# Inputs laid out anew on the host: linear attention with gates, queries and keys turned, token weights turned, and another order

## The chip, the core and the metric

The kernel runs on one core of a Trainium2 chip. The metric is the device time of one execution in microseconds; the layout of inputs on the host is not part of it. Names of engines: PE multiplies matrices, DVE, ACT and POOL work along rows, SP issues transfers.

## The reference

Four batches, 768 positions, 8 heads of 48 make 384 columns. Three networks follow one another: gated linear attention, softmax attention of four experts with a top-2 gate, and a token mixer with complex weights.

```python
def _attn_ref(q, k, v, f_logit):
    f = 1.0 / (1.0 + np.exp(-f_logit))
    for t in range(S):
        state = f[:, :, t, :, None] * state + np.einsum('bhd,bhe->bhde', k[:, :, t], v[:, :, t])
        y[:, :, t] = np.einsum('bhd,bhde->bhe', q[:, :, t], state)

def _moe_ref(x, w_gate, wq, wk, wv, wo):            # top 2 of 4 experts per token
    for e in range(E):
        a = softmax(causal(scale * (x @ wq[e]) @ (x @ wk[e]).T))
        out += weight_of_e * (a @ (x @ wv[e]) @ wo[e])

def _moe2_ref(x, w_theta, w_tok_r, w_tok_i, w_ch):
    theta = x @ w_theta
    y = w_tok_r @ (x * np.cos(theta)) + w_tok_i @ (x * np.sin(theta))
    u = x + y
    return u + np.maximum(u @ w_ch, 0.0)
```

The weights of the third network arrive as 64-bit numbers; the rest is float32.

## The kernel before, in words

Positions are cut into six tiles of 128 rows per batch, 24 tiles in all. Most products are made of two parts, a rounded high one and the low rest (names ending in h and l), with three products for one.

**Gla**, the linear attention. `load` brings a tile of gates (`g_f`), queries, keys and values, 128 positions on partitions, each row in runs of 48 numbers. `gate` makes logarithms of the gates on ACT and splits them (L289, L291); `cum` sums them along positions by two products with a triangle (L297, L298), takes exponentials both ways on ACT and scales keys and queries on DVE (L307, L308), and sends the decay at the tile's end through a small transfer to `g_end` (L310). `dec` turns that on PE (L324). `tr` turns keys and queries, four blocks each (L335), copied by ACT. `att` multiplies them (L348), POOL masks (L355). `out` sums values by the masked products (L366) and adds the running state's part (L370); ACT copies the result to `g_x`. `state` multiplies keys and values (L389) and updates the running state with DVE (L396, L398).

**Moe**, the softmax attention. `turn_x` turns the tile's output (L497) and splits it (`m_xh`, `m_xl`); `val` makes values and gate logits (L509), `qk` queries and keys of a pair of tiles (L556). Then 96 units (batch, expert, row tile): `score` (L604 to L607), maxima on DVE (L613), exponentials on ACT (L626), `turn` of the weights (L663) with split (L668, L675), `av` (L686, L688), `sum`, and `mix` (L723), which stores the third network's input `t_dram`.

**Weights** converts the 64-bit weights in pieces of 128 x 384 (four DVE steps L107 to L112 and one on ACT) and stores them (`w_f` to `w_dram`): 24 pieces of token weights, three of `w_ch`; three of `w_theta` stay on the chip.

**Late** and **Moe2**, the third network. `turn_rows` (L242) turns the token weights, 128 x 768 at a time, on PE and splits them from PSUM. `rot` makes the rotated inputs; `tok` multiplies (L824), `ch_a` and `ch_b` (L836, L847) finish. `Late` prepares most of the weights while the last units of the second network run.

What sets the order: `plan` gives every step a time from the table `TUNE`, sorts them, and the tool chain's scheduler places the instructions of each engine; PSUM has eight banks of one pool for all steps, and tiles in SBUF have fixed numbers of buffers. Each engine then works its instructions strictly in order; all transfers are issued by SP in order.

## Time and profile before

| | us |
|---|---|
| median of three runs | 684.59 (682.04 to 685.06) |
| the profiled execution | 685.65 |
| its span, first to last instruction | 683.9 |
| mean granted clock of PE | 0.983 |

Busy shares are taken over the whole span. A chain of waits is read backwards from the last instruction: at each point it names the work that the end waited for. [...]

### The profile page before, as it was taken

The numbers are of one execution on the slowest core, as the hardware profiler recorded it, in microseconds if no ns is written. First come the engines' busy times: TensorE is split into PE (matmuls) and PEld (weight loads), VectorE is DVE, ScalarE is ACT, GpSimd is POOL, SyncE is SP. The second block draws the span as 40 slices with busy tenths as digits, with TensorE's granted clock in tenths as the row PEclk, the third lists the DMA queues.
The fourth block names the chain that finished last, engine by engine and source line by source line (L and its number), as shares of the span: only waits on it lengthen the run. The fifth ranks groups of instructions, "written<-read, shape, count | busy, mean of one in ns | idle before, by whom it ended". The sixth has DMA issues, their size and how long they took to land.

```text
span 683.9 us, 13350 instructions
## 1 busy us (share of the span) xinstructions
PE 646.6 (95%) x4804; PEld 611.1 (89%) x4804; DVE 479.8 (70%) x1276; ACT 448.8 (66%) x1160; POOL 95.6 (14%) x118
## 2 busy tenths in 40 slices
PE   6999899999999999899999999999999999999995
PEld 5979789889889889899989998888999999999995
DVE  6289999999998999887777875987676244222221
ACT  4468778888888778887788776888877074040000
POOL 1410030000001010010000000001563042040000
PEclk8699999999999999999999999999999999999998
DMA  9387465363468264236121101245724121000110
GB/s 166 77 179 172 103 155 159 72 180 100 136 136 213 59 176 115 59 72 128 35 60 36 59 25 47 94 150 195 232 71 127 48 69 58 35 13 24 36 47 28
DMA packets 129562, 67.45 MB, mean 99 GB/s; under 512 B 107984, under 2 KB 120784, under 8 KB 129488
## 3 DMA queue, kind: packets, MB, share of 16 engines
q1 hardware_dynamic: 129488, 66.51, 37.9%
q8 instruction: 40, 0.66, 0.4%
q14 instruction: 34, 0.28, 0.1%
HBM read 47.00 MB, written 19.46 MB: 97 GB/s over the span
## 4 chain that ended last, share of the span: by engine, by line
PE 69%; DVE 17%; ACT 7%; DMA 3%; issue 3%; POOL 1%; DVEq 0%; SPq 0%; ACTq 0%; POOLq 0%
PE M L824 21%; PE M L723 6%; PE M L847 6%; PE M L366 5%; PE M L556 4%; PE M L348 3%; PE M L663 3%; PE M L370 2%; PE M L509 2%; PE M L335 2%; DVE m_m L613 2%; DVE m_al L675 2%; PE M L389 2%; PE M L604 2%; PE M L686 2%
## 5 line engine op out<-in xcount | busy, mean ns | idle before, releaser
L355 POOL TENSOR_SCALAR_AFFINE_SELECT g_a<-g_a 128x512 f32<-128x512 f32 x48 | 35.7, 761 | 360.4 <-ACT g_a L352 360.4
L626 ACT ACTIVATE m_a<-M,m_m 128x384 f32<-128x384 f32 (+4 forms) x128 | 69.9, 552 | 16.1 <-DVE m_m L613 9.5
L675 DVE TENSOR_TENSOR m_al<-M,m_ah 128x384 fp32r<-128x384 f32 (+3 forms) x128 | 62.4, 501 | 7.4 <-ACT m_ah L668 6.4
L613 DVE TENSOR_REDUCE m_m<-M 128x1 f32<-128x384 f32 (+4 forms) x128 | 62.2, 501 | 7.2 <-PE M L607 3.2
L94 ACT CAST t_uh<-M 128x384 fp32r<-128x384 f32 x24 | 11.4, 476 | 82.1 <-PE M L836 82.1
L663 PE MATMUL M<-c_ident,m_a 128*128 128x128 f32 x336 | 53.2, 275 | 4.7 <-DVE m_kl L578 4.0
L668 ACT CAST m_ah<-M 128x384 fp32r<-128x384 f32 (+3 forms) x128 | 53.4, 447 | 6.2 <-PE M L663 5.4
L366 PEld LDWEIGHTS M<-g_v,g_a 128*128 128x128 f32 x384 | 48.6, 203 | 3.2 <-POOL g_a L355 1.8
L366 PE MATMUL M<-g_v,g_a 128*128 128x48 f32 x384 | 49.7, 284 | 1.6 <-POOL g_a L355 1.0
L686 PE MATMUL M<-m_ah,m_v 128*128 128x256 f32 x192 | 48.1, 283 | 0.8 <-ACT m_ah L668 0.8
L824 PE MATMUL M<-t_z1h,t_w 128*128 128x384 f32 x138 | 46.6, 337 | 0.0
L95 DVE TENSOR_TENSOR t_ul<-M,t_uh 128x384 fp32r<-128x384 f32 x24 | 13.4, 557 | 44.5 <-ACT t_uh L94 44.4
L604 PE MATMUL M<-m_ks,m_qs 128*128 128x384 f32 (+4 forms) x128 | 44.1, 346 | 0.3 <-ACT m_a L626 0.3
L663 PEld LDWEIGHTS M<-c_ident,m_a 128*128 128x128 f32 x336 | 37.9, 141 | 6.9 <-PE M L607 3.0
L688 PE MATMUL M<-m_al,m_v 128*64 128x256 f32 x192 | 41.7, 266 | 0.7 <-DVE m_al L675 0.7
L605 PE MATMUL M<-m_kl,m_qs 128*128 128x384 f32 (+4 forms) x128 | 41.3, 324 | 0.3 <-DVE m_kl L578 0.3
L850 DVE SCALAR_TENSOR_TENSOR t_o<-M,t_u 128x384 f32<-128x384 f32 x24 | 13.4, 556 | 39.8 <-PE M L847 39.8
L129 POOL TENSOR_TENSOR t_z0l<-t_ra,t_z0h 128x384 fp32r<-128x384 f32 x23 | 24.3, 1058 | 98.3 <-ACT t_z0h L128 95.8
L686 PEld LDWEIGHTS M<-m_ah,m_v 128*128 128x128 f32 x192 | 36.2, 188 | 1.3 <-ACT m_ah L668 1.0
L723 PE MATMUL M<-m_wh,m_yh 128*128 128x384 f32 x96 | 34.7, 361 | 1.6 <-ACT m_yh L711 1.5
L723 PE MATMUL M<-m_wh,m_yl 128*128 128x384 f32 x96 | 32.4, 339 | 0.0
L723 PE MATMUL M<-m_wl,m_yh 128*128 128x384 f32 x96 | 32.3, 336 | 0.0
(245 smaller groups left out, 1994.5 us busy)
## 6 DMA issues: line engine op xcount, KB each, us to landing
t_dram<-m_xt SPq DMA_DIRECT2D x24, 384.0 KB
w_dram<-w_f SPq DMA_DIRECT2D x27, 192.0 KB
g_f<-in_f_logit_dram SPq DMA_DIRECT2D x24, 192.0 KB
g_k<-in_k_dram SPq DMA_DIRECT2D x24, 192.0 KB
g_q<-in_q_dram SPq DMA_DIRECT2D x24, 192.0 KB
g_v<-in_v_dram SPq DMA_DIRECT2D x24, 192.0 KB
w_d<-in_moe_w_tok_r_dram SPq DMA_DIRECT2D x12, 384.0 KB
w_d<-in_moe_w_tok_i_dram SPq DMA_DIRECT2D x12, 384.0 KB
```

Of the source, the lines that this page charges most:

```text
L366: nc.tensor.matmul(y[:, h * D:(h + 1) * D], t.a[:, r, hp, :], t.v[:, h * D:(h + 1) * D], start=h == 0, stop=c == 0, skip_group_check=True)
L604: nc.tensor.matmul(ps, qs[:, rows], ks[:, cols], start=True, stop=False)
L605: nc.tensor.matmul(ps, qs[:, rows], kl[:, cols], start=False, stop=not last)
L613: nc.vector.tensor_reduce(m, ps, axis=AX.X, op=OP.max, negate=True)
L626: self.nc.scalar.activation(a[:, cols], ps, AF.Exp, bias=t.m, accum_out=st.den[:, c, i % 2, e % 2:e % 2 + 1])
L663: nc.tensor.transpose(ps[:, (j - j0) * P:(j - j0 + 1) * P], t.a[:, j * P:(j + 1) * P], self.k.ident)
L668: nc.scalar.copy(hi, pv)
L675: self.nc.vector.tensor_tensor(lo, pv, hi.bitcast(F32), op=OP.subtract)
L686: nc.tensor.matmul(ps[:, o:TQ], st.v[j][:, e].rearrange("p c h -> p (c h)"), t.aT[0][:, j, o:], start=j == 0, stop=True, skip_group_check= ...
L688: nc.tensor.matmul(ps[:HD, o:TQ], st.v[j][:, e, 0, :], t.aT[1][:, j, o:], start=False, stop=True, skip_group_check=True)
L723: nc.tensor.matmul(ps[:, :DM], st.y[pr, t // 2][a][:, o], self.wl[c][:, 2 * w0 + pr, :], start=n == 0, stop=n == 5)
L824: nc.tensor.matmul(ps, self.wT[c][h][g][:, s, j * P:(j + 1) * P], self.Z[b, s][c][l], start=s == 0 and n == 0, stop=s == NT - 1 and n == 5)
```

## The change

Inputs are laid out on the host so that the first network needs less turning. Gates, queries and keys of a tile come turned: head columns on partitions (two heads of 48 in two halves of 64), positions along rows, 2 KB to a partition. The running sum of the gates' logarithms is then a scan along rows on DVE (`tensor_tensor_scan`, listed in the order as SCALAR_TENSOR_TENSOR), broken at the borders of four head pairs by `g_inside`. The decay at a tile's end is a column of that (`g_dec`), so the small transfer, the search for the least value and the turning go. Only keys are turned, for the state, and not in a batch's last tile. Outputs are made turned, in halves of 64 columns, from values padded to 64; the state is kept as a block with zeros (`g_block`), copied there by ACT. `turn_x` splits the product straight from PSUM; the fourth pair's columns (`m_x3`) go to their places by six transfers per tile on SP, and the rows of the experts' weights are laid out to suit. The token weights come turned, so `turn_rows` goes and the splits read SBUF. `w_o` also comes turned. Eight of twelve token pieces are prepared by `Late`, four by `Moe2` (before: nine and three). `TUNE` has other numbers, among them fewer warming products (46, 11 and 4 for 53, 25 and 6).

```diff
-N1 = 3
+NS0 = 4
...
-        elif it[0] == "turn":
-            _, c, t = it
-            turn_rows(self.nc, self.k, self.pM, self.raw.pop(it), [w[t // G] for w in self.wT[c]], t)
-
-
-def turn_rows(nc, k, pM, r, dst, t):
-
-    o = slice((t % G) * P, (t % G + 1) * P)
-    for h in range(2):
-        ps = pM.tile([P, 512], F32, name="M")
-        for j in range(G):
-            s = h * G + j
-            nc.tensor.transpose(ps[:, j * P:(j + 1) * P], r[:, s * P:(s + 1) * P], k.ident)
-        pv = ps[:, :DM].rearrange("p (j m) -> p j m", j=G)
-        split(nc, pv, dst[0][:, h * G:(h + 1) * G, o], dst[1][:, h * G:(h + 1) * G, o])
+        elif it[0] == "tok":
+            _, c, s = it
+            split(self.nc, self.raw.pop(it), self.wT[c][0][s], self.wT[c][1][s])
...
-        self.padded = dict(q=[], k=[])
-        for nm, n in (("q", 2), ("k", 3)):
-            for j in range(n):
-                w = self.wk.tile([P, H, HD], F32, name=f"g_{nm}{j}")
-                nc.vector.memset(w, 0.0)
-                self.padded[nm].append(w)
-        self.ends = []
-        for j in range(2):
-            w = self.wk.tile([P, 2, HD], F32, name=f"g_end{j}")
-            nc.gpsimd.memset(w, 1.0)
-            self.ends.append(w)
-        self.low = self.wk.tile([NP, B * NT], F32, name="g_low")
+        self.inside = self.wk.tile([P, NP, P], F32, name="g_inside")
+        nc.gpsimd.memset(self.inside, 1.0e30)
+        nc.gpsimd.memset(self.inside[:, :, 0:1], 0.0)
+        self.dec = self.wk.tile([P, B * NT, NP], F32, name="g_dec")
+        self.block, self.inblock = [], {}
+        for j in range(3):
+            w = self.wk.tile([P, NP, 2, HD], F32, name=f"g_block{j}")
+            nc.gpsimd.memset(w, 0.0)
+            self.block.append(w)
         self.states, self.ready = {}, {}
         self.T = {}
 
     def load(self, nm, b, c):
         t = self.T.setdefault((b, c), Bag())
-        if nm in "qk":
-            ws = self.padded[nm]
-            w = ws[(b * NT + c) % len(ws)]
-            dst = w[:, :, :D]
-        else:
-            w = self.wk.tile([P, DM], F32, name=f"g_{nm}", bufs=2)
-            dst = w.rearrange("p (h d) -> p h d", h=H)
-        self.nc.sync.dma_start(dst, self.src[nm][b, :, c * P:(c + 1) * P, :].rearrange("h t d -> t h d"))
-        setattr(t, nm + "raw" if nm in "qk" else nm, w)
+        w = self.wk.tile([P, H, HD] if nm == "v" else [P, NP, P], F32, name=f"g_{nm}", bufs=2)
+        self.nc.sync.dma_start(w, self.src[nm][b, c])
+        setattr(t, nm, w)
...
     def gate(self, b, c):
         nc, t = self.nc, self.T[b, c]
-        g = self.wk.tile([P, DM], F32, name="g_g")
-        nc.scalar.activation(g, t.f, AF.Exp, scale=-1.0)
-        nc.scalar.activation(g, g, AF.Ln, bias=1.0)
-        yield
-        t.gh = self.wk.tile([P, DM], F32R, name="g_gh")
-        nc.vector.tensor_scalar(t.gh, g, GCLAMP, None, op0=OP.min)
-        t.gl = self.wk.tile([P, DM], F32R, name="g_gl")
-        nc.vector.scalar_tensor_tensor(t.gl, g, GCLAMP, t.gh.bitcast(F32), op0=OP.min, op1=OP.subtract)
+        nc.scalar.activation(t.f, t.f, AF.Exp, scale=-1.0)
+        nc.scalar.activation(t.f, t.f, AF.Ln, bias=1.0)
+        yield
+        t.cum = self.wk.tile([P, NP, P], F32, name="g_cum")
+        flat = lambda a: a.rearrange("p n t -> p (n t)")
+        nc.vector.tensor_tensor_scan(flat(t.cum), flat(self.inside), flat(t.f), initial=0.0, op0=OP.min, op1=OP.add)
 
     def cum(self, b, c):
         nc, t = self.nc, self.T[b, c]
-        i = b * NT + c
-        ps = self.pM.tile([P, 512], F32, name="M")
-        nc.tensor.matmul(ps[:, :DM], self.k.upper_r, t.gh, start=True, stop=False)
-        nc.tensor.matmul(ps[:, :DM], self.k.upper_r, t.gl, start=False, stop=True)
-        yield
-        ei = self.wk.tile([P, DM], F32, name="g_ei")
-        nc.scalar.activation(ei, ps[:, :DM], AF.Exp)
-        e = self.wk.tile([P, DM], F32, name="g_e", bufs=2)
-        nc.scalar.activation(e, ps[:, :DM], AF.Exp, scale=-1.0)
-        yield
-        heads = lambda a: a.rearrange("p (h d) -> p h d", h=H)
-        k, q = t.kraw[:, :, :D], t.qraw[:, :, :D]
-        (nc.vector if i < 2 or TUNE['e_k'] else nc.gpsimd).tensor_tensor(k, k, heads(ei), op=OP.mult)
-        (nc.vector if i < 2 or TUNE['e_q'] else nc.gpsimd).tensor_tensor(q, q, heads(e), op=OP.mult)
-        t.k, t.q, t.end = t.kraw, t.qraw, self.ends[i % 2].rearrange("n j d -> n (j d)")
-        nc.sync.dma_start(self.ends[i % 2][:NP, :, :D], e[P - 1:P, :].rearrange("p (n j d) -> p n j d", n=NP, j=2))
-
-    @staticmethod
-    def pair(a, hp):
-        return a[:, 2 * hp:2 * hp + 2, :].rearrange("p h d -> p (h d)")
-
-    def dec(self, b, c):
+        ei = self.wk.tile([P, NP, P], F32, name="g_ei")
+        nc.scalar.activation(ei, t.cum, AF.Exp)
+        e = t.f
+        nc.scalar.activation(e, t.cum, AF.Exp, scale=-1.0)
+        yield
+        nc.vector.tensor_tensor(t.k, t.k, ei, op=OP.mult)
+        nc.vector.tensor_tensor(t.q, t.q, e, op=OP.mult)
+        (nc.vector if TUNE['e_dec'] else nc.gpsimd).tensor_copy(self.dec[:, b * NT + c, :], e[:, :, P - 1])
...
-        nc.vector.tensor_copy(t.dec[:, :, 0], ps[:, :NP])
-
-    def tr(self, b, c):
-        nc, t = self.nc, self.T[b, c]
-        bank = {}
-        for nm in "kq":
-            ps = bank[nm] = self.pM.tile([P, 512], F32, name="M")
-            for hp in range(NP):
-                nc.tensor.transpose(ps[:, hp * P:(hp + 1) * P], self.pair(getattr(t, nm), hp), self.k.ident)
-        yield
-        for nm, ps in bank.items():
-            sb = self.wk.tile([P, NP, P], F32, name=f"g_{nm}T")
-            (nc.vector.tensor_copy if TUNE['e_' + nm + 'T'] else nc.scalar.copy)(sb.rearrange("p n t -> p (n t)"), ps)
-            setattr(t, nm + "T", sb)
+        for hp in range(NP):
+            nc.tensor.transpose(ps[:, hp * P:(hp + 1) * P], t.k[:, hp, :], self.k.ident)
+        yield
+        t.kn = self.wk.tile([P, H, HD], F32, name="g_kn")
+        (nc.vector.tensor_copy if TUNE['e_kn'] else nc.scalar.copy)(t.kn.rearrange("p h d -> p (h d)"), ps)
...
-                nc.tensor.matmul(ps[:, hp, :], t.kT[r, hp, :], t.qT[r, hp, :], start=True, stop=True)
+                nc.tensor.matmul(ps[:, hp, :], t.k[r, hp, :], t.q[r, hp, :], start=True, stop=True)
...
-        y = self.pM.tile([P, 512], F32, name="M")
-        for r in range(2):
+        y = self.pM.tile([P, NP, P], F32, name="M")
+        for hp in range(NP):
+            for r in range(2):
+                nc.tensor.matmul(y[64 * r:64 * r + 64, hp, :], t.v[:, 2 * hp + r, :], t.a[:, r, hp, :],
+                                 start=hp == 0, stop=c == 0, skip_group_check=True)
+        if c > 0:
+            assert self.inblock[(b * NT + c - 1) % 3] == (b, c)
+            bd = self.block[(b * NT + c - 1) % 3].rearrange("p n r d -> p n (r d)")
             for hp in range(NP):
-                h = 2 * hp + r
-                nc.tensor.matmul(y[:, h * D:(h + 1) * D], t.a[:, r, hp, :], t.v[:, h * D:(h + 1) * D],
-                                 start=h == 0, stop=c == 0, skip_group_check=True)
-        for hp in range(NP):
-            if c > 0:
-                nc.tensor.matmul(y[:, hp * 96:(hp + 1) * 96], t.qT[:, hp, :], self.states[b][:, hp, :],
-                                 start=False, stop=True, skip_group_check=True)
+                nc.tensor.matmul(y[:, hp, :], bd[:, hp, :], t.q[:, hp, :], start=False, stop=True, skip_group_check=True)
         t.used = True
-        yield
-        x = self.x[b, c] = self.wk.tile([P, DM], F32, name="g_x")
-        (nc.vector.tensor_copy if TUNE['e_x'] else nc.scalar.copy)(x, y[:, :DM])
+        self.x[b, c] = y
...
-            st = self.states[b] = self.wk.tile([P, NP, 96], F32, name="g_state", bufs=2)
-            nc.gpsimd.memset(st, 0.0)
+            self.states[b] = self.wk.tile([P, NP, D], F32, name="g_state", bufs=2)
         st = self.states[b]
         ps = self.pM.tile([P, 512], F32, name="M")
-        kv = ps.rearrange("p (n t) -> p n t", n=NP)
+        kv = ps[:, :NP * D].rearrange("p (n d) -> p n d", n=NP)
         for hp in range(NP):
-            nc.tensor.matmul(kv[:HD + D, hp, :96], self.pair(t.k, hp)[:, :HD + D], t.v[:, hp * 96:(hp + 1) * 96], start=True, stop=True)
-        yield
+            for r in range(2):
+                nc.tensor.matmul(kv[64 * r:64 * r + 64, hp, :], t.kn[:, 2 * hp + r, :], t.v[:, 2 * hp + r, :D],
+                                 start=hp == 0, stop=True, skip_group_check=True)
+        yield
+        src = kv
+        if c > 0:
+            nc.vector.tensor_tensor(st, src, st, op=OP.add)
+            src = st
+        dec = self.dec[:, b * NT + c, :].rearrange("p (n o) -> p n o", o=1).to_broadcast([P, NP, D])
+        nc.vector.tensor_tensor(st, src, dec, op=OP.mult)
+        bd = self.block[(b * NT + c) % 3]
+        self.inblock[(b * NT + c) % 3] = (b, c + 1)
         for r in range(2):
-            rows = slice(64 * r, 64 * r + D)
-            sl = st[rows, :, r * D:(r + 1) * D]
-            src = kv[rows, :, r * D:(r + 1) * D]
-            if c > 0:
-                nc.vector.tensor_tensor(sl, src, sl, op=OP.add)
-                src = sl
-            nc.vector.tensor_tensor(sl, src, t.dec[rows].to_broadcast([D, NP, D]), op=OP.mult)
+            rows = slice(64 * r, 64 * r + 64)
+            (nc.scalar.copy if TUNE['e_bd'] else nc.gpsimd.tensor_copy)(bd[rows, :, r, :D], st[rows])
...
-            st.xs[h] = tuple(self.xp.tile([P, KT, TQ], F32R, name=f"m_x{n}", bufs=2) for n in "hl")
+            st.xs[h] = self.xp.tile([P, 2, KT, TQ], F32R, name="m_xs", bufs=2)
+        xs = st.xs[h]
         x = self.x.pop((b, t))
-        ps = self.pM.tile([P, 512], F32, name="M")
-        for j in range(KT):
-            nc.tensor.transpose(ps[:, j * P:(j + 1) * P], x[:, j * P:(j + 1) * P], self.k.ident)
-        yield
-        split(nc, ps[:, :DM].rearrange("p (j m) -> p j m", j=KT), st.xs[h][0][:, :, o], st.xs[h][1][:, :, o])
-        st.xT[t] = st.xs[h]
+        if x.shape[1] == NP:
+            last = self.xp.tile([P, 2, P], F32R, name="m_x3", bufs=2)
+            nc.scalar.copy(xs[:, 0, :, o], x[:, :KT])
+            nc.scalar.copy(last[:, 0], x[:, KT])
+            yield
+            nc.vector.tensor_tensor(xs[:, 1, :, o], x[:, :KT], xs[:, 0, :, o].bitcast(F32), op=OP.subtract)
+            nc.vector.tensor_tensor(last[:, 1], x[:, KT], last[:, 0].bitcast(F32), op=OP.subtract)
+            for j in range(KT):
+                for r in range(2):
+                    rows = slice(64 * r + 16 * j, 64 * r + 16 * j + 16)
+                    nc.sync.dma_start(xs[64 * r + D:64 * r + 64, :, j, o].bitcast(F32), last[rows].bitcast(F32))
+        else:
+            ps = self.pM.tile([P, 512], F32, name="M")
+            for j in range(KT):
+                nc.tensor.transpose(ps[:, j * P:(j + 1) * P], x[:, j].rearrange("p r d -> p (r d)"), self.k.ident)
+            yield
+            split(nc, ps[:, :DM].rearrange("p (j m) -> p j m", j=KT), xs[:, 0, :, o], xs[:, 1, :, o])
+        st.xT[t] = (xs[:, 0], xs[:, 1])
...
-    def w_load(self, c, t):
-        r = self.W[c, t] = self.pp.tile([P, S], F32, name="t_wr", bufs=G)
-        self.nc.sync.dma_start(r, self.rows.tok[c][t * P:(t + 1) * P, :])
-
-    def w_turn(self, c, t):
-        turn_rows(self.nc, self.k, self.pM, self.W.pop((c, t)), [w[1] for w in self.wT[c]], t)
+    def w_load(self, c, s):
+        r = self.W[c, s] = self.pp.tile([P, S], F32, name="t_wr", bufs=G)
+        self.nc.sync.dma_start(r, self.rows.tok[c][s * P:(s + 1) * P, :])
+
+    def w_split(self, c, s):
+        split(self.nc, self.W.pop((c, s)), self.wT[c][0][s], self.wT[c][1][s])
...
-        tm = g["tok0"] + n * (g["tok1"] - g["tok0"]) / len(tok)
+        tm = g["tok0"] + (n / len(tok)) ** g["tok_p"] * (g["tok1"] - g["tok0"])
...
+    def turned(a, fill):
+        w = np.full((B, NT, 2, HD, NP, P), fill, a.dtype)
+        w[:, :, :, :D] = a.reshape(B, NP, 2, NT, P, D).transpose(0, 3, 2, 5, 1, 4)
+        return w.reshape(B, NT, P, NP, P)
+
+    v = np.zeros((B, NT, P, H, HD), src["v"].dtype)
+    v[..., :D] = src["v"].reshape(B, H, NT, P, D).transpose(0, 2, 3, 1, 4)
...
+        woT=np.ascontiguousarray(w["wo"].reshape(E * HD, DM).T), w_theta=words(w2["w_theta"]),
+        w_tok_r=words(w2["w_tok_r"].T), w_tok_i=words(w2["w_tok_i"].T), w_ch=words(w2["w_ch"]))
```

What this moves is shown at three places. The first is PE at the outputs of tile 3 of the second batch (M is a bank of PSUM, m_ names belong to the second network). Before:

```order
L663 MATMUL M<-c_ident,m_a 128x128 x6
L366 MATMUL M<-g_v,g_a 128x48 x8
L370 MATMUL M<-g_state,g_qT 128x96 x4
L389 MATMUL M<-g_v,g_k_104 112x96 x4
L509 MATMUL M<-w_vgh,m_xh 128x260 x3
L509 MATMUL M<-w_vgl,m_xh 128x260 x3
L509 MATMUL M<-w_vgh,m_xl 128x260 x3
L497 MATMUL M<-c_ident,g_x 128x128 x3
```

and now:

```order
L484 MATMUL M<-w_vgl,m_xs 128x260 x3
L484 MATMUL M<-w_vgh,m_xs 128x260 x3
L317 MATMUL M<-g_a,g_v 64x128 x8
L323 MATMUL M<-g_q,g_block_108 128x128 x4
L339 MATMUL M<-g_v,g_kn 64x48 x8
L580 MATMUL M<-m_ks,m_qs 128x128
L581 MATMUL M<-m_kl_125,m_qs 128x128
```

The outputs change from a 128-wide held operand and 48 moving columns to 64 held and 128 moving, the state's products double in number, and the turning of `g_x` is gone from behind them.

The second is DVE around the gates of a tile in the same batch. Before:

```order
L307 TENSOR_TENSOR g_k_108<-g_k_108,g_ei 128x8x48
L308 TENSOR_TENSOR g_q_100<-g_q_100,g_e 128x8x48
L613 TENSOR_REDUCE m_m<-M 128x1 x2
L675 TENSOR_TENSOR m_al<-M,m_ah 128x3x128
L616 TENSOR_TENSOR m_m<-m_m 128x1
L675 TENSOR_TENSOR m_al<-M,m_ah 128x2x128
L320 TENSOR_REDUCE g_low<-g_end_110 4x1
L289 TENSOR_SCALAR g_gh<-g_g 128x384
```

and now:

```order
L344 TENSOR_TENSOR g_state<-M,g_state 128x192
L269 SCALAR_TENSOR_TENSOR g_cum<-g_inside,g_f 128x512
L347 TENSOR_TENSOR g_state<-g_state,g_dec 128x192
L462 TENSOR_TENSOR m_xs<-M,m_xs 128x3x128
L463 TENSOR_TENSOR m_x_1823<-M,m_x_1823 128x128
L109 SCALAR_TENSOR_TENSOR w_b<-w_d,w_b 128x384
L589 TENSOR_REDUCE m_m<-M 128x1 x2
L118 SCALAR_TENSOR_TENSOR m_xt<-m_k,M 128x384
```

The scan `g_cum` stands where the two halves of the gates stood, the output is split from PSUM without a turning between, and steps of the conversion (`w_b`) stand among them. Of the 27 stored pieces (`w_f`) 26 stand before unit 48 in the order before, 18 now.

The third is SP's queue in that batch. Before:

```order
L180 DMA w_dram<-w_f 128x384
L310 DMA g_end_112<-g_e 4x2x48
L279 DMA g_f<-in_f_logit_dram 128x8x48
L734 DMA t_dram<-m_xt 128x768
L279 DMA g_q_102<-in_q_dram 128x8x48
```

and now:

```order
L259 DMA g_q<-in_qT_dram 128x512
L259 DMA g_v<-in_vp_dram 128x512
L467 DMA m_xs<-m_x_1823 16x2x128 x6
L711 DMA t_dram<-m_xt 128x768
L100 DMA w_d<-in_w_tok_i_dram 128x768
L259 DMA g_f<-in_fT_dram 128x512
L178 DMA w_dram<-w_f 128x384
```

The small transfer of the decay's end is gone; six transfers of 16 partitions each (`m_xs`) stand between the loads and stores.

## Rows read from the trace of the kernel before

**Rows 1.** The page, busy time of each engine, and packets of all transfers.

```profile
PE 646.6 (95%) x4804; PEld 611.1 (89%) x4804; DVE 479.8 (70%) x1276; ACT 448.8 (66%) x1160; POOL 95.6 (14%) x118
...
DMA packets 129562, 67.45 MB, mean 99 GB/s; under 512 B 107984, under 2 KB 120784, under 8 KB 129488
```

**Rows 2.** S1 to S5: stretch, its length, busy us (records), clock, transfers.

```profile
0.00:51.70 51.70, 44.18 (x316) 39.44 (x317) 31.97 (x83) 28.30 (x63) 12.58 (x26) 0.80 0.80 142
51.70:269.80 218.10, 206.24 (x1739) 192.38 (x1737) 205.57 (x578) 179.50 (x484) 22.35 (x28) 1.00 0.54 137
269.80:433.20 163.40, 157.86 (x1312) 147.68 (x1310) 125.74 (x375) 127.10 (x352) 9.99 (x16) 1.00 0.24 57
433.20:491.30 58.10, 52.78 (x363) 47.74 (x363) 45.20 (x116) 49.47 (x130) 10.61 (x10) 1.00 0.54 177
491.30:684.00 192.70, 185.57 (x1080) 183.88 (x1079) 71.34 (x128) 64.41 (x135) 40.11 (x38) 0.99 0.17 55
```

**Rows 3.** Chain of waits at full clock: start us, length us, work.

```profile
209.37 0.18 PE M L297
...
240.06 1.09 PE M L348 x16
244.69 1.77 PE M L366 x16
246.47 0.93 PE M L370 x8
247.40 0.79 PE M L389 x8
...
471.94 2.63 PE M L242 x24
```

**Rows 4.** DVE by line and form: operands, count, busy us, mean ns, idle before.

```profile
L307 DVE TENSOR_TENSOR g_k<-g_k,g_ei 128x384 f32<-128x384 f32 x24 | 13.2, 552 | 0.8 <-ACT g_ei L301 0.6
L291 DVE SCALAR_TENSOR_TENSOR g_gl<-g_g,g_gh 128x384 fp32r<-128x384 f32 x24 | 13.2, 548 | 0.5
L396 DVE TENSOR_TENSOR g_state<-M,g_state 48x192 f32<-48x192 f32 x32 | 11.3, 353 | 6.1 <-PE M L389 5.4
L675 DVE TENSOR_TENSOR m_al<-M,m_ah 128x512 fp32r<-128x512 f32 x16 | 11.0, 689 | 0.7 <-ACT m_ah L668 0.4
L289 DVE TENSOR_SCALAR g_gh<-g_g 128x384 fp32r<-128x384 f32 x24 | 9.9, 411 | 2.3 <-ACT g_g L286 1.8 <-PE M L298 0.4
L320 DVE TENSOR_REDUCE g_low<-g_end 4x1 f32<-4x128 f32 x24 | 6.4, 265 | 1.1 <-DMA g_end<-g_e 1.1
L675 DVE TENSOR_TENSOR m_al<-M,m_ah 128x128 fp32r<-128x128 f32 x16 | 4.6, 285 | 1.2 <-ACT m_ah L668 1.1
```

**Rows 5.** Stretches of the steps of the conversion alone (tile w_b).

```profile
0.00:684.00 684.00, 64.16 (x120) 0.98 0.38 99
```

**Rows 6.** Chain of waits in S1.

```profile
1.15 0.48 DVE g_q L259
11.58 4.36 DMA m_ks<-in_moe_wq_dram
18.73 3.59 PE M L366 x16
24.51 0.90 PE M L497 x3
36.27 0.63 PE M L335 x4
38.37 0.33 PE M L759 x3
```

**Rows 7.** Timeline of one small transfer and its reader; SP's waits (total, times, longest).

```profile
33.44 0.66 SPq L310 DMA_DIRECT2D g_end<-g_e  x1
36.51 0.27 DVE L320 TENSOR_REDUCE g_low<-g_end 4x1 f32<-4x128 f32 x1
...
SPq L279 <- PE M L389: 40.0, 11, 12.2
```

174 lines of the change are left out of this document (79 added, 95 removed).

## The prediction

> **What bounds the kernel now.** I read the page's busy times first: PE 95%, DVE 70%, ACT 66% [rows 1]. Those are averages over unlike stretches, so I cut the span at five marks: the first score product (51.7 us), that of unit 48 (269.8), that of unit 88 (433.2), and the point where the last network's products run without gaps (491.3). I call the pieces S1 to S5 [rows 2]. The reader is to see three things there. In S5 PE is busy throughout while DVE and ACT have more than half their time free; the change hardly touches that work. In S2 two engines are full at once: PE 206.24 and DVE 205.57 of 218.1 us, 94.6% and 94.3%. In S3 PE is full alone: 157.86 of 163.4 us, 96.6%, with DVE at 125.74. So in S2 a gain on PE is only worth what DVE also sheds; in S3 DVE has some 38 us to spare. [...]
>
> Durations of PE records overlap, so PE is priced by the distance of neighbours on the chain of waits [rows 3]: a turning of 128 columns 0.11 us (24 in 2.63), a decay product 0.18, the attention products of a tile 1.09, the outputs 1.77, the state's share of them 0.93, the state's own products 0.79.
>
> **The change on PE, per tile (24 tiles; three outputs fall in S1, 13 in S2, 8 in S3).** Gone: two decay products, 0.36; the turning of the decay's end, 0.11 in five tiles of six, 0.09; eight turnings of keys and queries become four in five tiles of six, 0.88 to 0.37, so 0.51; three turnings of the output, 0.33. Together 1.29.
>
> Three groups change shape. The outputs are now eight products with 64 columns held and 128 moving, alternating between the lower and the upper half of the output. No row has that shape. The nearest is the attention group: same count, same 128 moving columns, alternating halves of the input rows, 1.09 [rows 3]. If column halves overlap as those row halves do, the group falls from 1.77 to 1.09 (-0.68); if not, each product costs twice that row's share and the group 2.18 (+0.41). I take 1.09, the row it is nearest to, and keep both ends. The state's share moves 128 columns instead of 96: between 0.93 and 0.93 x 128/96 = 1.24, in five of six tiles 0 to +0.26; I take +0.1. The state's products are eight of 64 columns instead of four of 112: held columns grow from 448 to 512, so 0.79 becomes 0.90; if each of the eight costs what one costs today, 1.58; 0 to +0.66 per tile, I take +0.1. Sum per tile: -1.29 - 0.68 + 0.1 + 0.1 = **-1.77**, ends -1.97 and 0.
>
> **On DVE, per tile.** Gone [rows 4]: the two halves of the gates 0.411 + 0.548, the search for the least decay 0.265, keys, queries and the output's low part at 0.552 each, and the state's steps, four of 0.353 in four tiles of six and two in one, 1.06 on average: 3.94 in all. Come in: keys and queries at 512 columns, 2 x 0.689; half as many state steps, 0.53; the output's low part 0.552 and its last quarter 0.285; that is 2.75. Then the scan over 512 columns. No row shows one. As one pass over two inputs it costs 0.689, twice that is 1.378. Each element needs the result before it, which none of the passes in the rows does, so I take 1.378 and keep both ends. Sum per tile: **+0.18**, at the other end -0.51.
>
> [...]
>
> The order moves another load. A piece of the conversion from 64 bits holds DVE for 64.16 / 30 = 2.14 us [rows 5]. Before unit 48 stand 26 of the 27 stored pieces now, 18 in the changed order; eight pieces, 17 us, go from S2 to S3.
>
> ACT: the copies of the queries (512 columns) and of the output (384) go; four exponentials and logarithms grow by 128 columns each, a quarter of 128 and two copies of 192 come. That is 128 columns more per tile on an engine at 179.5 of 218.1 us in S2 and 127.1 of 163.4 in S3 [rows 2]; DVE hides it, and if that cover is gone it costs under 0.2 us a tile.
>
> **SP and the transfers.** The six new transfers per tile (144) stand in SP's queue behind the loads and stores around them; they wait for DVE's low part, and the next tile's loads wait behind them. Today's nearest are the 24 small transfers of the decay's end: issue 0.66 us, read 3.1 us after their issue began [rows 7]. Six issues and that landing make 4 + 2.4 = 6.4 us at most from the low part; the first products of values and of queries need them. In the changed PE order the work between a tile's outputs and the first product that needs them is at least 10.9 us for all tiles from the fifth to the 23rd, so those hide it. Among the first four it is 3.2 us at the least, for the last 5.1: I charge S1 with 2 us, since a low clock stretches the cover, and the last tile with nothing.
>
> **Sum by stretch.** S1, by its own rows [rows 6], which are taken partly at the low clock: the clearing of five padded tiles on DVE, the first work of the chain, 5 x 0.54 = 2.6 us (0.48 each and the gap to the next). On PE one turning of an output, 0.90; of two output groups the first stood at 3.59 and would at the low clock be 2 x 1.09 = 2.18, 1.4 less, and I count 1.1 for the second; a turning of queries, 0.63; two turnings of a late weight, 0.33 each. That is 6.9; less 2 for the transfers: **-5**. The wait of 4.36 us for the first weights [rows 6] lies behind loads in runs of 192 bytes (107984 of 129562 packets are under 512 B [rows 1]); those become runs of 2 KB. I count nothing for it and keep -9 as the end.
>
> S2, scan dear: DVE 205.57 - 17 + 12 x 0.18 = 190.7; at today's share of 94.3%, 202.3 us, **-15.8**. PE would allow 206.24 - 13 x 1.77 = 183.2, at 94.6% 193.7. DVE decides.
>
> S3: DVE 125.74 + 17 + 8 x 0.18 = 144.2, at 94.3% 152.9 us, **-10.5**; PE 157.86 - 8 x 1.77 = 143.7, at 96.6% 148.8. DVE is late next here too, as PE's stall goes.
>
> S4: all 72 turnings of the token weights go, 72 x 0.11 = 7.9 us, of which 24 in a row stand on the chain, 2.63 [rows 3]. The splits on ACT and DVE keep their columns, and what those engines owe the first products there is not PE's. I take **-3**, ends 0 and -7.9. S5: 0.
>
> Total -5 - 15.8 - 10.5 - 3 = -34.3. The profiled execution took 685.65 us (span 683.9 and 1.75 around it): 651.35. The median, 684.59, lies 1.06 lower: **650**.
>
> **Rivals.**
> 1. The scan is a single pass. DVE per tile -0.51: S2 DVE 182.4, so 193.5 (-24.6), level with PE; S3 falls to PE's 148.8 (-14.6). Total -47, **637**. For it: the row of one pass; against it: the carried result.
> 2. Column halves do not overlap: outputs 2.18, per tile -0.68. S2 PE 197.4, 208.7 us (-9.4); S3 152.4, 157.8 (-5.6); S1, where the two groups now cost more, -1; S4 -3. Total -19, **665.5**. With the state's products at 1.58 as well, PE gains nothing per tile, -4 in all: about **680.5**. For it: row halves are what the row shows, column halves are not.
> 3. Slower: SP's queue. A load that waits for its buffer holds the queue; the rows show 11 waits of the loads on the state's products, the longest 12.2 us [rows 7]. Behind such a wait six transfers land 12.2 + 6.4 = 18.6 us after their data, 5 to 8 us past the cover of the last tile of a pair (10.9 to 13.8 us in the middle batches), and PE stands. It decides from 34.3 us over 12 pairs, 2.9 us each, a landing of some 14 us in every pair; at 6 us in all pairs the time is 650 + 72 = 722, in two thirds of them **698**. Against it: the loads are released earlier when the order is less tight, and their issue is the same in number.
> 4. Nothing moves, because conversions on DVE that now lie in S3 delay the maxima there by what S2 gains: **684**. Against it: 38 us free in S3 [rows 2].
>
> **How the numbers follow.** Chances: the forecast 0.56; rival 1 0.14; rival 2 0.19, of which 0.03 for 680.5; rival 3 0.04; rival 4 0.03; a start that stays longer at the low clock, some 657, 0.04. The range runs from 635, rival 1 with the better start, to 670, rival 2 with a poorer one. About 0.5% is what a measurement of this kernel can tell from no change: faster 0.93, same 0.03, slower 0.04.
>
> **What would show it.** Right: units 0 to 48 in about 202 us and 48 to 88 in about 153, DVE busier than PE in the second; a scan near 1.3 us; output groups of 16 near 1.09 on the chain; waits of PE on the six transfers only in the first tiles. Wrong: scans near 0.7 (rival 1), output groups near 2 us (rival 2), PE idle before the products of queries, released by SP's transfers (rival 3), long waits of ACT's exponentials on DVE in S3 (rival 4).

## The result, and the profile after

| | before | after |
|---|---|---|
| median, us | 684.73 (682.04 to 685.06, 4 runs) | 664.03 (663.09 to 666.77, 4 runs) |
| ratio of the means | | 0.9713 (95%: 0.9674 to 0.9751) |
| the profiled execution / its span | 685.65 / 683.9 | 664.45 / 662.7 |
| mean granted clock of PE | 0.983 | 0.964 |

The kernel is faster by 20.7 us where 34.6 were forecast: inside the range, nearest to rival 2's 665.5 though not by rival 2's mechanism. The page of the changed kernel, busy times and packets, answers to [rows 1]; the third line is the scan's group, as the groups by line and form list it (count, busy us, mean ns, idle before).

```profile
PE 603.5 (91%) x4611; PEld 553.9 (84%) x4611; DVE 481.5 (73%) x1203; ACT 453.8 (68%) x1159; POOL 102.1 (15%) x117
...
DMA packets 46682, 76.45 MB, mean 115 GB/s; under 512 B 6672, under 2 KB 25616, under 8 KB 46608
...
L269 DVE TENSOR_TENSOR_SCAN g_cum<-g_inside,g_f 128x512 f32<-128x512 f32 x24 | 30.3, 1263 | 5.4 <-ACT g_f L265 4.9 <-ACT g_f L276 0.3
```

PE lost 43 us of busy time and half of that came back as time in which it stands. The stretches S1, S2, S3 and the rest (S4 and S5 in one), cut at the same score products as [rows 2], same columns:

```profile
0.00:46.80 46.80, 33.80 (x282) 28.37 (x283) 32.34 (x63) 29.38 (x63) 16.91 (x27) 0.74 0.62 198
46.80:262.70 215.90, 193.54 (x1696) 169.75 (x1695) 199.17 (x536) 183.61 (x493) 22.23 (x26) 0.97 0.46 140
262.70:415.50 152.80, 144.04 (x1262) 129.98 (x1261) 132.05 (x380) 126.86 (x353) 11.10 (x16) 0.99 0.33 103
415.50:662.70 247.20, 232.09 (x1379) 225.83 (x1377) 117.97 (x227) 113.97 (x253) 51.81 (x48) 0.99 0.27 86
```

| stretch | forecast | measured |
|---|---|---|
| S1 | -5 | 51.7 to 46.8: -4.9 |
| S2 | -15.8 | 218.1 to 215.9: **-2.2** |
| S3 | -10.5 | 163.4 to 152.8: -10.6 |
| S4 and S5 | -3 | 250.8 to 247.2: -3.6 |

So the question is S2. PE is busy for 12.7 us less there, yet the stretch is 2.2 us shorter: PE's idle time went from 11.9 to 22.4 us, and its clock, at 1.00 throughout S2 before [rows 2], is 0.97. What PE waited for in S2 of the changed kernel (us in total, times, longest):

```profile
PE M L317 <- POOL g_a L307: 5.2, 6, 1.7
PE M L532 <- DMA m_xs<-m_x: 2.9, 3, 1.7
PE M L580 <- DVE m_kl L554: 2.7, 2, 1.4
PE M L581 <- DVE m_kl L554: 2.6, 2, 1.3
PE M L662 <- DVE m_al L651: 1.7, 2, 1.1
PE M L662 <- ACT m_ah L644: 1.4, 1, 1.4
```

No single wait is long; they are many, and behind different engines. One of them in full, the timeline around 116 us (start us, length us, work, idle before and its releaser):

```profile
115.50 0.62 ACT L274 ACTIVATE g_ei<-g_cum 128x512 f32<-128x512 f32 x1
116.12 0.37 ACT L549 CAST m_ks<-M 64x256 fp32r<-64x256 f32 x1
...
116.95 0.31 PE L581 MATMUL M<-m_kl,m_qs 128*128 128x320 f32 x1
...
117.26 0.37 ACT L551 CAST m_ks<-M 64x256 fp32r<-64x256 f32 x1
...
117.66 0.86 DVE L554 TENSOR_TENSOR m_kl<-M,m_ks 64x256 fp32r<-64x256 f32 x2 [0.57 <-ACT m_ks L551]
...
118.66 0.39 PE L580 MATMUL M<-m_ks,m_qs 128*128 128x320 f32 x1 [1.41 <-DVE m_kl L554]
...
120.68 0.68 DVE L651 TENSOR_TENSOR m_al<-M,m_ah 128x512 fp32r<-128x512 f32 x1
...
121.42 0.58 PE L662 MATMUL M<-m_ah,m_v 128*128 128x256 f32 x1 [1.08 <-DVE m_al L651]
```

PE stands 1.41 us for the keys' low part; DVE, which makes it, stands 0.57 us itself, for ACT's fourth copy of the keys; ACT did an exponential of the first network ahead of those copies. Then PE stands again, 1.08 us, while DVE has the state, the next output's split and two maxima ahead of the low part that PE needs. No one engine is full throughout (ACT is from 116 to 118 us, DVE from 118 to 122, in the rows below): the work is a string through three in-order queues. The stretches of 2 us there show what follows on PE (columns as above: the first busy time is PE's, the third number from the end the clock):

```profile
114.00:116.00 2.00, 2.00 (x27) 1.74 (x25) 1.85 (x6) 1.94 (x5) 0.00 (x0) 1.00 0.45 137
116.00:118.00 2.00, 1.26 (x11) 0.93 (x9) 1.40 (x3) 1.93 (x6) 0.00 (x0) 1.00 0.66 211
118.00:120.00 2.00, 1.04 (x7) 0.74 (x8) 1.96 (x7) 1.12 (x4) 0.00 (x0) 1.00 0.65 208
120.00:122.00 2.00, 0.92 (x4) 0.68 (x5) 2.00 (x6) 1.66 (x6) 0.00 (x0) 0.59 0.10 25
122.00:124.00 2.00, 2.00 (x12) 2.00 (x12) 1.32 (x5) 1.30 (x6) 0.00 (x0) 0.50 0.11 25
```

PE was busy for 1.26 and for 1.04 of two stretches of 2 us; in the next the clock fell from 1.00 to the lower level, 0.50 (0.59 is the mean of the stretch in which it fell). This happens three times in S2, 13.7 us in all.

### The profile page after: what moved, and what is told of

The parts are those of the page before. It is cut to its first block, busy times and chain, and to the rows that moved or that the text cites. A ratio compares the mean times of both kernels' runs of the same rounds, so it can differ in the third digit from the quotient of the medians.

```text
span 662.7 us, 13073 instructions
## 1 busy us (share of the span) xinstructions
PE 603.5 (91%) x4611; PEld 553.9 (84%) x4611; DVE 481.5 (73%) x1203; ACT 453.8 (68%) x1159; POOL 102.1 (15%) x117
## 5 line engine op out<-in xcount | busy, mean ns | idle before, releaser
L307 POOL TENSOR_SCALAR_AFFINE_SELECT g_a<-g_a 128x512 f32<-128x512 f32 x48 | 37.6, 804 | 336.1 <-ACT g_a L304 336.1
L639 PE MATMUL M<-c_ident,m_a 128*128 128x128 f32 x336 | 55.8, 282 | 4.5 <-DVE m_x L463 1.4
L662 PE MATMUL M<-m_ah,m_v 128*128 128x256 f32 x192 | 51.0, 295 | 6.0 <-DVE m_al L651 2.8
L580 PE MATMUL M<-m_ks,m_qs 128*128 128x384 f32 (+4 forms) x128 | 48.1, 377 | 5.2 <-DVE m_kl L554 3.0
L664 PE MATMUL M<-m_al,m_v 128*64 128x256 f32 x192 | 44.0, 275 | 1.5 <-DVE m_al L651 1.5
L317 PE MATMUL M<-g_a,g_v 128*64 128x128 f32 x384 | 32.9, 293 | 9.1 <-POOL g_a L307 9.1
L317 PEld LDWEIGHTS M<-g_a,g_v 128*64 128x64 f32 x384 | 24.1, 144 | 15.2 <-POOL g_a L307 12.2
L269 DVE TENSOR_TENSOR_SCAN g_cum<-g_inside,g_f 128x512 f32<-128x512 f32 x24 | 30.3, 1263 | 5.4 <-ACT g_f L265 4.9
L580 PEld LDWEIGHTS M<-m_ks,m_qs 128*128 128x128 f32 x128 | 24.8, 194 | 10.5 <-issue 3.3
L128 ACT CAST t_z0h<-t_ra 128x384 fp32r<-128x384 f32 x23 | 11.7, 508 | 31.5 <-PE M L797 28.1
```

Source lines behind the costliest of these rows:

```text
L317: nc.tensor.matmul(y[64 * r:64 * r + 64, hp, :], t.v[:, 2 * hp + r, :], t.a[:, r, hp, :], start=hp == 0, stop=c == 0, skip_group_check=True)
L580: nc.tensor.matmul(ps, qs[:, rows], ks[:, cols], start=True, stop=False)
L639: nc.tensor.transpose(ps[:, (j - j0) * P:(j - j0 + 1) * P], t.a[:, j * P:(j + 1) * P], self.k.ident)
L662: nc.tensor.matmul(ps[:, o:TQ], st.v[j][:, e].rearrange("p c h -> p (c h)"), t.aT[0][:, j, o:], start=j == 0, stop=True, skip_group_check= ...
L664: nc.tensor.matmul(ps[:HD, o:TQ], st.v[j][:, e, 0, :], t.aT[1][:, j, o:], start=False, stop=True, skip_group_check=True)
```

## The experiments

Theories that the expectations name: **A**, DVE's load decides S2; **B**, PE's work and its waits for single chains add up, whatever DVE's load; **C**, the six transfers hold SP's queue; **D**, PE that stands falls to the low clock and loses by it; **E** (formed after the first eight runs), S2 is set by strings of work that pass in order through the queues of several engines. Times are medians with their extremes; the changed kernel's is 664.03 (663.09 to 666.77). The windows below are always S2 and, where shown, S3, in the columns of [rows 2].

**x1, one pass instead of the scan.** The order of every engine is that of the changed kernel.

```diff
-        nc.vector.tensor_tensor_scan(flat(t.cum), flat(self.inside), flat(t.f), initial=0.0, op0=OP.min, op1=OP.add)
+        nc.vector.tensor_tensor(flat(t.cum), flat(self.inside), flat(t.f), op=OP.min)
```

> The scan is replaced by one pass of the same two inputs over the same 512 columns (the lesser of both), so the running sum of the decays is left out; the order of every engine stays as it is. The scan took 1.26 us, one pass at 512 columns some 0.70, so DVE sheds 0.56 x 24 = 13.5 us, 7.8 of them in S2 (14 scans of the changed kernel stand there). Theory A, DVE's load decides S2 (199.2 of 215.9 us, a share of 92.3%): S2 falls to (199.2 - 7.8) / 0.923 = 207.4 us, and the whole by 9 to 11, to about 654. Theory B, PE waits there for single chains of steps (the split of queries and keys at the end of each pair, the masks) and then runs at the low clock, whatever DVE's load: S2 moves by under 2 us, the whole by under 3. Theory C, the six transfers in SP's queue hold PE: no change.

Measured: 656.85 (656.26 to 657.38), 7.2 us less than the changed kernel; ratio to before 0.9588 (0.9553 to 0.9623).

```profile
45.30:254.20 208.90, 190.41 (x1695) 167.34 (x1694) 191.89 (x536) 182.65 (x493) 20.24 (x26) 0.98 0.47 143
254.20:408.10 153.90, 145.75 (x1261) 131.46 (x1261) 130.17 (x380) 126.79 (x353) 11.11 (x16) 0.98 0.33 103
```

S2 gives back 7.0 us for 7.3 us off DVE: as A said, a little less. Theory C has no place for it, B hardly. But the scan is also a link in the first network's chain, so x5 takes the same load off elsewhere.

**x2, queries and the decay's end on POOL.**

```diff
-        nc.vector.tensor_tensor(t.q, t.q, e, op=OP.mult)
+        (nc.vector if b * NT + c < 2 else nc.gpsimd).tensor_tensor(t.q, t.q, e, op=OP.mult)
...
-    e_dec=1
+    e_dec=0
```

> The scaling of the queries (0.75 us on DVE) and the copy of the decay's end (0.24) go to POOL from the third tile on, the result being the same. DVE sheds 0.99 x 13 = 13 us in S2 and 9 more behind it. Theory A: DVE at 186 us falls below PE, and S2 is then PE's, (193.5 less some 4 of low clock) / 0.966 = 196 to 200 us, the whole at about 646. Theory B: POOL needs some 1.4 us for what DVE did in 0.75 and the attention products and masks come later; S2 moves by less than 3 us either way, the whole 661 to 667. Theory C: no change.

Measured: 681.67 (678.89 to 685.68), 17.6 us slower than the changed kernel; none of the theories said that. The first fence shows two of DVE's groups by form, the state's decay L347 and the state's sum L344, the second S2:

```profile
L347 DVE TENSOR_TENSOR g_state<-g_state,g_dec 128x192 f32<-128x192 f32 x16 | 7.8, 486 | 0.1
L344 DVE TENSOR_TENSOR g_state<-M,g_state 128x192 f32<-128x192 f32 x16 | 5.6, 352 | 0.6 <-ACT g_block L352 0.2 <-PE M L339 0.2
```

```profile
45.00:270.50 225.50, 199.08 (x1696) 173.77 (x1695) 201.83 (x515) 184.42 (x494) 43.13 (x54) 0.95 0.45 138
```

DVE's load did not fall: 201.8 us. Two things that the trace shows filled it up: some steps took longer beside POOL (L347, on average 348 ns in the changed kernel, now 486), and the order that came with the edit put 84 records of the conversion in S2 instead of 74. POOL's product took 1.37 us against 0.75 on DVE. So x2 does not test A.

**x3, output halves one after the other.**

```diff
-        for hp in range(NP):
-            for r in range(2):
+        for r in range(2):
+            for hp in range(NP):
                 nc.tensor.matmul(y[64 * r:64 * r + 64, hp, :], ...
```

> The eight output products of the lower column half stand first and those of the upper half behind them, instead of in turns; all else is the same. If column halves overlap only where neighbours use different halves, a group of 16 goes from 1.02 us to about 2, by the 0.126 of a product that stands alone; if the halves do not matter, it stays at 1.02 and the time at 664. With a dearer group: theory A, S2 is DVE's and takes up most of the 13 us that PE gets more, under +4 there, +8 in S3 where PE is full, the whole about 674. Theory B, PE's work and its waits add up: +13 in S2 too, the whole about 686.

Measured: 665.00 (661.89 to 667.27), no different. A group of 16 and its followers in the changed kernel, then such a group in x3 (timelines of PE; the price is the distance of two starts), and S2 of x3:

```profile
112.55 1.09 PE L317 MATMUL M<-g_a,g_v 128*64 128x128 f32 x16
113.58 1.16 PE L323 MATMUL M<-g_q,g_block 128*128 128x128 f32 x8
114.66 0.67 PE L339 MATMUL M<-g_v,g_kn 128*64 128x48 f32 x16
```

```profile
112.27 1.58 PE L317 MATMUL M<-g_a,g_v 128*64 128x128 f32 x16
113.78 1.16 PE L323 MATMUL M<-g_q,g_block 128*128 128x128 f32 x8
```

```profile
46.70:259.60 212.90, 196.53 (x1697) 174.53 (x1696) 198.17 (x536) 183.05 (x492) 22.39 (x26) 0.98 0.46 142
```

1.03 us against 1.51 (the median of 18 such groups): halves in turns overlap, and in blocks they lose a part of that, not all. Yet 0.49 us more per tile, 12 us over the kernel, cost nothing that can be measured. Against B: S2 is not PE's any more.

**x4, the six transfers from POOL's queue.**

```diff
-                    nc.sync.dma_start(xs[64 * r + D:64 * r + 64, :, j, o]...
+                    nc.gpsimd.dma_start(xs[64 * r + D:64 * r + 64, :, j, o]...
```

> The six transfers per tile that bring the fourth pair's columns to their places are issued by POOL instead of SP. SP waited 58.6 us on DVE's low part at their head in the changed kernel, and loads stand behind them. Theory C: with that gone the loads come earlier, PE's 6.1 us of waits on the transferred columns go, and the whole falls by 6 or more, to 658 or less. Theories A and B: SP had slack, the time stays within 2 us of 664, or grows a little by POOL's issues ahead of the masks.

Measured: 671.59 (671.06 to 674.15), 7.6 us slower, 6.2 of it in S3 (159.0 us); S2 217.4. PE's waits on the six transfers did not go: 6.1 us in the changed kernel, 9.5 here. The order changed with it, so the loss can't be laid to POOL alone. No gain: C finds no support.

**x5, a cheaper conversion.**

```diff
-    nc.vector.scalar_tensor_tensor(t, hi, -0x40000000, t, op0=OP.bitwise_and, op1=OP.bitwise_or)
-    nc.vector.scalar_tensor_tensor(t, lo, 29, t, op0=OP.logical_shift_right, op1=OP.bitwise_or)
+    nc.vector.tensor_scalar(t, t, 0, None, op0=OP.bitwise_or)
+    nc.vector.tensor_scalar(t, t, 0, None, op0=OP.bitwise_or)
```

> In the changed kernel, two of the four DVE steps of a conversion piece (0.58 and 0.60 us, two inputs) become steps with one input of the same size (0.37): the top bits of the exponent and the lowest three bits of each converted weight are left out. Nobody but the store waits for these steps, so this takes load off DVE without shortening any chain of the first two networks: 0.44 x 30 = 13 us in all, 8 of them in S2, as much as x1 took away. Theory A, load: S2 shortens by 4 to 8 us and the whole comes to 655 to 659, as with x1. Rival, the scan's place in the chain of gates, scaling and keys was what x1 gained by: S2 and the whole stay within 2 us of the changed kernel.

Measured: 663.26 (662.59 to 666.53), no different.

```profile
47.20:260.60 213.40, 193.13 (x1695) 169.36 (x1693) 194.46 (x545) 184.70 (x495) 21.14 (x26) 0.98 0.47 145
260.60:414.80 154.20, 146.12 (x1262) 132.38 (x1263) 126.46 (x371) 125.64 (x351) 12.30 (x16) 0.97 0.30 97
```

DVE has 11.7 us less work over the kernel, 4.7 in S2 (two more pieces came to stand there), and the time is the same; S2 is 2.5 us shorter, S3 1.4 longer. A's 655 to 659 did not come. But the order of DVE and ACT moved with this edit (545 records of DVE in S2 for 536), so what the order took back isn't known, and x5 alone doesn't refute A.

**x6, three groups by halves.** As x3, also in `att` (`for j` outside `for hp`) and in `state`.

> As x3 for the outputs, and the attention products and the state's products are also set half by half instead of in turns. x3 made the outputs dearer by 0.49 us a tile (1.51 against 1.02) at no cost in time; this adds some 0.5 for the attention products and 0.3 for the state's, 1.3 us a tile, 31 us of PE work in all. Theory A with D (DVE's load decides S1 and S2, and PE stands and then falls to the low clock): most of it goes into time in which PE stood or ran at the low clock; S2 grows by under 5 us, S3, where PE is full, by up to 9; the whole 664 to 676, with less time at the low clock than the 48 us of the changed kernel. Theory B, PE's work counts: +31, about 693.

Measured: 676.14 (675.68 to 677.29).

```profile
49.80:266.70 216.90, 204.35 (x1695) 183.42 (x1693) 197.24 (x530) 182.35 (x489) 20.59 (x26) 0.98 0.45 134
266.70:426.00 159.30, 153.12 (x1262) 139.43 (x1263) 135.17 (x386) 128.00 (x355) 10.92 (x16) 0.99 0.33 105
```

The whole is at the upper end of what A with D allowed, far from B's 693, and the time at the low clock went down to about 39 us, as D said. In S2 10.8 us more PE work cost 1.0 us; in S3 9.1 us more cost 6.5 (in x3 2.2 us more there had cost 0.1). So S3 reads as still largely PE's, and in S2 PE has room; the order moved here too, unlike in x3.

**x7, the numbers of before with the new layout.** 68 of the 76 numbers of `TUNE` that both kernels have go back, and `tok_p=1`.

> The changed kernel with the numbers of the plan's table from before, for all keys that both have, and the conversions spread evenly again: the layout alone, without the order anew. On DVE 20 stored pieces stand ahead of unit 48 then, for 18 in the changed kernel and 26 before, and 14 scans as in the changed one. Theory A: S2 is longer by 2 x 2.14 = 4 us, the whole about 668 to 672. If the order anew carries the gain: 680 or more. If it is worth nothing: 664.

Measured: 676.88 (674.72 to 680.16). S1, S2 and S3:

```profile
0.00:50.40 50.40, 36.23 (x294) 30.66 (x294) 35.16 (x71) 31.08 (x66) 16.52 (x27) 0.76 0.56 182
50.40:266.50 216.10, 195.03 (x1706) 171.94 (x1705) 197.21 (x530) 180.79 (x487) 21.77 (x26) 0.95 0.47 145
266.50:427.60 161.10, 148.43 (x1269) 132.87 (x1269) 131.04 (x374) 128.15 (x357) 11.85 (x16) 0.98 0.30 94
```

The time lies between A's 668 to 672 and the 680 of a gain by the order alone. With the old numbers the layout gives 8 us (685.1 to 676.9), the order anew 12.8: 3.6 in S1, 8.3 in S3, and nothing in S2, which is 216 us long in either order. It also tells how much an order is worth with the same work; where an edit moved the order too (x2, x4 to x6 and x9 to x11), a few us either way can't be laid to the edit.

**x8, the kernel before with the token weights turned.** `Late` and `Moe2` as in the change, and on the host:

```diff
-        a = _np.ascontiguousarray(inputs[name])
+        a = _np.asarray(inputs[name])
+        a = _np.ascontiguousarray(a.T if "w_tok" in name else a)
```

> The kernel before with the token weights alone laid out turned (no turning on PE, splits from SBUF, eight of twelve pieces prepared early), all else as before. The prediction's term for this is -3 us (0 to -7.9): 682 against 685. If the turnings stood wholly beside other work: no change. If all 72 counted: 677.

Measured: 682.68 (678.40 to 683.70) against 685.10 in the same runs, ratio 0.9955 (0.9934 to 0.9975): -2.4. S1 to S3 are within 0.2 us of before; the rest went from 250.8 to 247.9 us:

```profile
433.20:681.10 247.90, 232.12 (x1370) 225.16 (x1369) 119.55 (x231) 113.95 (x252) 51.36 (x48) 0.98 0.26 84
```

**x9, a third buffer for the gates.** Theory E came from following the waits back from the score product of unit 48, by the rule of the chain of waits (the chain on the page stops at 475 us). Over S2 of the changed kernel that string runs 87 us through DVE, 50 through ACT, 32 through transfers and their issue and only 26 through PE; before, 115 through PE, 72 through DVE and 11 through ACT. Three loads of gates stand in it, 12.0 us; the scan has 7.3 us of it, and the DVE steps of the conversion have 15.0, because they stand in DVE's queue ahead of work that is waited for.

```diff
-        ... name=f"g_{nm}", bufs=2)
+        ... name=f"g_{nm}", bufs=3 if nm == "f" else 2)
...
-        t.cum = self.wk.tile([P, NP, P], F32, name="g_cum")
+        t.cum = t.f
```

> The changed kernel with three buffers for the gates' tiles instead of two; the scan writes over its input to make room. Theory E: with PE lighter, S2 is set by strings of work that pass in order through loads, ACT, DVE and SP's transfers; followed back from unit 48, three loads of gates stand in the string with 12 us of the 215.9. If so S2 shortens by 4 to 10 us and the whole comes to 654 to 660. If the load of DVE alone decides (theory A), the same work in another order gives 660 to 668.

Measured: 666.91 (665.39 to 668.72), above E's 654 to 660. S2:

```profile
44.50:264.00 219.50, 195.42 (x1697) 171.90 (x1696) 195.48 (x530) 180.33 (x488) 21.76 (x26) 0.96 0.45 135
```

Followed back in the same way, loads of gates now have 6.8 us of the string and other work the rest: the loads were in it but were not what holds it. The order moved too. **A falls here**, as the whole account: with 195.5 us on DVE S2 took 219.5 us, and in x5 with 194.5 it took 213.4 (the clock 0.96 and 0.98).

**x10, the output split in one step.** `m_xs` gets a fourth block that takes the place of `m_x3`; one copy and one subtraction of 512 columns; the decay's end copied by `nc.scalar.copy`; `t.cum = t.f`.

> The changed kernel with one copy and one subtraction of 512 columns for a tile's turned output, instead of 384 and 128 apart (DVE 0.55 + 0.28 becomes 0.69), the copy of the decay's end on ACT (0.24 off DVE), and the scan over its input. The result is the same. DVE sheds 0.38 x 24 = 9 us, 5 of them in S2, and a bank of PSUM comes free one step sooner. Theories A and E both: shorter by 3 to 8 us, 656 to 661, faster than both kernels. If the order that comes with it weighs more than the work: within 5 us of 664 either way.

Measured: 668.02 (666.85 to 669.41), 4 us slower than the changed kernel with 8 us less work on DVE (S2 214.8, S3 155.5). A and E had both said 656 to 661, and both missed; what the order that came with it cost isn't known.

**x11, the decay's end on ACT.**

```diff
-        (nc.vector if TUNE['e_dec'] else nc.gpsimd).tensor_copy(self.dec[:, b * NT + c, :], e[:, :, P - 1])
+        nc.scalar.activation(self.dec[:, b * NT + c, :], t.cum[:, :, P - 1], AF.Exp, scale=-1.0)
```

> The changed kernel with the decay at a tile's end made by ACT from the scan's last column (one exponential of four columns) instead of copied by DVE (0.24 us, 24 times). PE's order stays but for a few rows. Theory A: S2's DVE loses 15 x 0.24 = 3.6 us, the whole 660 to 662. Theory E: the copy is one short step behind the scaling of the queries, off most strings: 662 to 666.

Measured: 666.57 (664.58 to 667.61), just above E's 662 to 666 and further above A's 660 to 662; S2 215.2. The order of DVE and ACT moved.

**x12, x5 and x1 together.** Every engine's order is that of x5.

> x5 and x1 together: the cheaper conversion, and one pass in place of the scan; every engine's order is that of x5, as x1's was that of the changed kernel. The running sum of the decays and some bits of the converted weights are left out. Against x5 DVE sheds 0.53 x 14 = 7.4 us in S2. If S2 is set by strings of work in which the scan itself stands, the gain of x1 comes again: S2 from 213.5 to about 206, the whole from 663.3 to 655 to 657. If x5 gained so little because S2 rests on something else than DVE below some 195 us of its load: S2 211 or more, the whole 660 or more. By DVE's load at the share of before, 0.943, it would be 187 / 0.943 = 198 us, and the whole 648.

Measured: 658.49 (656.34 to 659.27), 4.8 us less than x5; S1 gave 2.6 of it and S2, in the profiled execution, 2.5:

```profile
44.60:255.50 210.90, 193.90 (x1696) 171.40 (x1694) 187.99 (x545) 184.25 (x495) 19.15 (x26) 0.96 0.48 147
```

Two times, from the changed kernel to x1 and from x5 to x12, the scan's extra half microsecond was taken away with the order unchanged, 12 us of DVE over the kernel each time; it gave 7.2 and 4.8 us. Two times the conversion was made cheaper by as much, with the order moved; it gave 0.8 us (the changed kernel to x5: 664.03 to 663.26) and cost 1.6 (x1 to x12: 656.85 to 658.49). Shown by the first two pairs is the scan's price. Why the conversion's differs is not shown: x5's expectation said that nobody but the store waits for it, but it has 15.0 us of the string of x9, twice the scan's share, and what the order took back is not known. That the scan's price acts through strings is E's reading, which x9 and x10 did not bear out. S2 between the expected 206 and 211 decides nothing more.

No version of these beats the changed kernel with the same result. Not tried: filler products that keep PE busy through its waits without another order; so what the low clock costs by itself stays open. The executions of one kernel give an upper hint: among 13 of the kernel before, 681.32 us at a mean clock of 0.992 and 687.20 at 0.980, 0.36 us per us at the low clock (span x (1 - clock) x 2, as the lower level is 0.50 of the upper: 11 and 27 us); of the changed kernel 663.09 at 0.972 and 666.77 at 0.963, 0.30. The changed kernel spends 48 us there and the kernel before 23, so by this estimate up to 8 us of the missing gain may hang on it; a longer stall would raise both numbers, though, and in S1 x11 had the full clock throughout and was only 2.6 us shorter.

## Why the prediction was right or wrong

**S1, -5: right in size, not in its parts.** With the old numbers the layout gave 1.3 us (x7, 50.4); 3.6 came with the order anew, which the sum did not count. That the total fits is luck. The factor of two at the low clock was an estimate: in S1 of the kernel before the clock was 0.50 from 18.73 to 22.32 us, where a group of outputs took 3.59 us against 1.77 at 1.00 [rows 3]; a group of the new shape at the low clock was not measured apart.

**PE per tile: near where the clock was full.** The outputs were forecast at 1.09 and measured 1.03, so column halves overlap as the row halves of [rows 3] do, and rival 2's mechanism is refuted although the time fell on its number. The state's share came to 1.08 (forecast 0.93 plus 0.1), the state's own products to 0.60 (0.79 plus 0.1). In S3 PE lost 13.8 us where 8 x 1.77 = 14.2 had been forecast. In S2 it lost 12.7 where 13 x 1.77 = 23.0 had been: 13.7 us there were at the lower clock, which by an estimate (PE busy throughout, all of it twice as long at a clock of 0.50) adds up to 6.9 us of busy time; the rest is open.

**DVE per tile: near, too.** The scan took 1.263 us; the dear end, 1.378, was the right choice against 0.689, and rival 1 falls. That a scan costs twice a pass was an estimate, and no row of before showed a scan; against the single pass over the same inputs, 0.730 in x1, it took 1.73 times. Keys and queries took 0.716 and 0.750 for 0.689. The copy of the decay's end, 0.241, had been left out, as had its forerunner.

**S2, -15.8: here the prediction failed**, at "DVE decides", in two steps. First the load: 190.7 forecast, 199.2 measured. The conversion left as forecast, 26 stored pieces before and 18 now. But I multiplied the tile's balance by 12 tiles, and the order anew puts the first network further ahead: the rows of S2 for one tile's name, the scan now (DVE, then ACT's exponentials that read it; the first scan is cut by the edge) and the two halves of the gates before (PE, PEld, then DVE, two to a tile):

```profile
46.80:262.70 215.90, 18.44 (x15) 18.66 (x30) 0.97 0.46 140
```

```profile
51.70:269.80 218.10, 4.87 (x12) 2.27 (x12) 11.19 (x24) 1.00 0.54 137
```

Fourteen scans begin in S2 where twelve gates did; the order, which was at hand, shows the same. Summed over durations, the first network's steps on DVE are 4.8 us above the forecast by that and by their prices, the conversion 1.9 and the second network's 2.2: 8.9 together. Second, the share: 94.3% was held to be DVE's ceiling, so that S2 would follow its load. DVE's share fell to 92.3% instead, and x9 and x5, 1 us apart in DVE's load, were 6 us apart in S2. Of the 13.6 us that S2 fell short, the load makes about 9 at the old share, the share under 5. Before, PE and DVE were full together; now neither is (89.6% and 92.3%). x3 shows that S2 isn't set by PE's work alone, x9 beside x5 that it isn't set by DVE's load alone; x1 and x12 show that the scan has a price in it. What does set it stays open: that strings of work through DVE, ACT, POOL and SP do is how the waits read, and x9 and x10, which were to show it, missed. The prediction had asked only which of two loads is next, not how long the waits between them are.

**S3, -10.5: the size right by luck, the reason wrong.** DVE was to be busier than PE there and to decide, 144.2 us. It is at 132.1 (five scans begin there, and eight tiles had been counted) and PE at 144.0, 94% of 152.8. With the old numbers S3 stays at 161.1 (x7): 8.3 of the 10.6 us come from the order, for which no gain had been forecast.

**S4, -3: right**, measured apart in x8 at -2.4 (-2.9 in S4 and S5 of the profiled execution): about a third of the 7.9 us of turnings was on the path.

**Rivals 3 and 4.** PE waited 6.1 us for the six transfers in eight places, not only in the first tiles as forecast but nowhere long; no slower case came of it. Rival 4 was half right: in S2 nothing moved, but not because the conversions went to S3.
